# The first channel product of two more batches in 11 products for 12

## The chip, the cores and the metric

The kernel runs on one core of a Trainium2 chip. The metric is the device time of one execution in microseconds (us), as a median of several runs; the profile comes from one execution of its own. TensorE (PE) multiplies, VectorE (DVE) and ScalarE (ACT) work on what it leaves in PSUM, GpSimd (POOL) clears buffers and starts some transfers, SyncE (SP) starts the others. Each engine takes its instructions strictly in the order in which the program gives them.

## The reference

All arrays are float32: 4 batches, 8 heads, 768 tokens, head size 48, so 384 values per token.

```python
def attn(q, k, v, beta):                      # for each batch and head
    k_n = k / (norm(k) + 1e-6)
    for t in range(768):
        y[t] = q[t] @ state                   # state: 48 x 48
        v_old = state.T @ k_n[t]
        state = state + beta[t] * outer(k_n[t], v[t] - v_old)

x = y                                         # (batch, 768, 384), heads side by side
h = x.transpose(0, 2, 1) @ U @ V              # mixes tokens, rank 32
u = x + h.transpose(0, 2, 1)
ch = maximum(u @ w_ch1, 0) @ w_ch2            # 384 -> 1536 -> 384
out = u + ch
```

## The kernel before, in words

**Attention.** The recurrence is worked in chunks of 64 tokens. The eight (batch, half of the tokens) units n0 to n7 go through `grams` (transposes and products of keys and queries), `blocks` (a triangular substitution on VectorE, a chain of pairs of instructions, lines 803 and 809, between transposes at lines 794 and 816), `joins` (small products that put blocks of 32 together to 64) and `prepare`. `recur(b)` then runs over the twelve chunks of a batch, with the `z` subtraction (line 1085) and the state addition (line 1111) on VectorE between its products.

**Mixer.** For each batch b and each tile i of 256 tokens, `front(b, i)` mixes the tokens into X (line 1417) and transposes the tile (line 1436), and ScalarE copies it to `ut` (line 1439, two buffers). `wide(b, i)` then makes two channel products:

- The first, 384 to 1536, in `channels(e)` for e = 0 to 5 (batches 0 to 2). Each takes two of the twelve column blocks f of w_ch1, three matmuls of 128x128 weights by 256 tokens for each (line 1497). PSUM bank `mix` 0 or 1 holds the result; ScalarE applies relu into `hs` (line 1462, 512 columns at once).
- The second, 1536 to 384, in `narrow(e)` (line 1617): seven products in place of eight, by sums of the halves of `hs` (`add_up`, line 1524, and `last_sum`) and of the weights. `gather` adds the results to X (line 1537), SyncE stores them.

The last batch, b = 3, is different already: `quick(f)` makes its first product for all 768 tokens in 11 matmuls for 12, of 384 columns (line 1296). It uses sums of weights, made by `weight_sums` (lines 1256 and 1264: n1, s2 and s4, and a21 replaced by a11 - a21), and sums of the transposed tokens (`token_sums`, line 1280). Of each f and its partner f + 6, four results c(k, m) are built up: products run on in PSUM, ScalarE copies a state of the sum out (lines 1314, 1318, 1323), VectorE adds another product to it (line 1305), ScalarE applies relu (line 1300).

**Order.** Every function is a generator that gives one step of one engine at a time: `op(engine, cost, mode, take, give)`. A string named ORDER lists, for each generator, the places of its steps in the whole program; `run()` gives out the instructions in exactly that order. `need(...)` says which events have to have been given out before; `take` and `give` hand PSUM banks on. The cost in an `op` is a note of the program to itself, and no instruction depends on it. Modes say how TensorE's array is used: F is whole (128x128), Q is 64x64 or 48x64 parts, J 32x32 parts, T 128x32.

Of the kernel before, what the change touches and what calls it, by code (L numbers as in the profile page):

```python
# [20 lines left out]
GT = 256  # L21
# [6 lines left out]
def kernel(  # L28
# [66 lines left out]
    def dve(n):  # L95
        return (n + 151) / 960.0
# [48 lines left out]
    add_up b0 i0 f00: 573 585 613; add_up b0 i0 f03: 645 676 690; add_up b0 i1 f00: 795 797 800; add_up b0 i1 f03:  # L145
    818 819 824; add_up b0 i2 f00: 942 944 1042; add_up b0 i2 f03: 1023 1051 1071; add_up b1 i0 f00: 1161 1166 1186;
    add_up b1 i0 f03: 1189 1190 1191; add_up b1 i1 f00: 1309 1337 1363; add_up b1 i1 f03: 1357 1359 1368; add_up b1
    i2 f00: 1488 1493 1571; add_up b1 i2 f03: 1564 1572 1576; add_up b2 i0 f00: 1695 1717 1737; add_up b2 i0 f03:
    1728 1729 1730; add_up b2 i1 f00: 1888 1895 1906; add_up b2 i1 f03: 1886 1889 1901; add_up b2 i2 f00: 1992 2000
    2026; add_up b2 i2 f03: 2046 2047 2049; add_up b3 i0 f00: 2185 2186 2188; add_up b3 i0 f03: 2191 2192 2195;  # L150
    add_up b3 i1 f00: 2201 2202 2207; add_up b3 i1 f03: 2208 2209 2210; add_up b3 i2 f00: 2227 2228 2236; add_up b3
    i2 f03: 2224 2225 2229; blocks n0: 61 73 75 76 82 84 86 88 89 91 93 94 96 97 103 110 114 122; blocks n1: 143 157
    160 163 173 175 179 192 201 206 208 212 213 215 218 219 226 229; blocks n2: 479 496 501 502 508 512 513 514 515
    516 518 519 525 532 534 536 539 542; blocks n3: 704 720 721 729 730 733 739 741 761 765 769 771 772 773 778 779
    780 781 783 785 786 787 791 798 801 802 813 815 823 828 829 834 836 838; blocks n4: 971 982 985 987 989 996 1007
    1009 1012 1036 1038 1039 1040 1064 1074 1077 1082 1083 1087 1090 1107 1116 1119 1120 1122 1127 1129 1131 1132
    1133 1137 1138 1139 1140; blocks n5: 1168 1195 1198 1207 1218 1225 1227 1230 1231 1236 1241 1244 1249 1259 1269
    1271 1276 1278 1281 1286 1288 1291 1293 1294 1298 1311 1313 1314 1316 1323 1324 1332 1333 1351; blocks n6: 1510
    1523 1532 1541 1547 1558 1563 1566 1567 1568 1569 1596 1603 1612 1616 1617 1620 1622 1624 1645 1649 1653 1660
    1663 1665 1666 1671 1672 1673 1674 1675 1681 1684 1699; blocks n7: 1713 1724 1725 1739 1741 1744 1757 1762 1767  # L160
    1773 1775 1780 1782 1783 1800 1806 1807 1810 1817 1824 1829 1834 1837 1838 1849 1850 1856 1857 1860 1865 1866
    1867 1879 1881; both f0: 2149; both f1: 2105; both f2: 2147; both f3: 2123; both f4: 2111; both f5: 2184;
    channels b0 i0 e0: 546 547; channels b0 i0 e1: 549 550; channels b0 i0 e2: 552 553; channels b0 i0 e3: 567 574;
    channels b0 i0 e4: 588 591; channels b0 i0 e5: 604 633; channels b0 i1 e0: 768 776; channels b0 i1 e1: 777 788;
    channels b0 i1 e2: 790 792; channels b0 i1 e3: 799 803; channels b0 i1 e4: 806 807; channels b0 i1 e5: 808 814;
    channels b0 i2 e0: 898 899; channels b0 i2 e1: 907 912; channels b0 i2 e2: 935 936; channels b0 i2 e3: 950 959;
    channels b0 i2 e4: 965 969; channels b0 i2 e5: 995 1005; channels b1 i0 e0: 1118 1130; channels b1 i0 e1: 1136
    1148; channels b1 i0 e2: 1150 1151; channels b1 i0 e3: 1153 1155; channels b1 i0 e4: 1156 1158; channels b1 i0
    e5: 1159 1175; channels b1 i1 e0: 1297 1299; channels b1 i1 e1: 1300 1302; channels b1 i1 e2: 1304 1305; channels
    b1 i1 e3: 1306 1307; channels b1 i1 e4: 1326 1327; channels b1 i1 e5: 1342 1343; channels b1 i2 e0: 1430 1431;  # L170
    channels b1 i2 e1: 1432 1449; channels b1 i2 e2: 1450 1469; channels b1 i2 e3: 1470 1497; channels b1 i2 e4: 1498
    1501; channels b1 i2 e5: 1516 1530; channels b2 i0 e0: 1650 1654; channels b2 i0 e1: 1656 1669; channels b2 i0
    e2: 1686 1687; channels b2 i0 e3: 1689 1692; channels b2 i0 e4: 1697 1698; channels b2 i0 e5: 1700 1701; channels
    b2 i1 e0: 1808 1812; channels b2 i1 e1: 1813 1831; channels b2 i1 e2: 1833 1841; channels b2 i1 e3: 1843 1869;
    channels b2 i1 e4: 1871 1873; channels b2 i1 e5: 1874 1876; channels b2 i2 e0: 1950 1959; channels b2 i2 e1: 1960
    1961; channels b2 i2 e2: 1973 1979; channels b2 i2 e3: 1987 1999; channels b2 i2 e4: 2011 2027; channels b2 i2
    e5: 2033 2037; copies f0: 2127 2136; copies f1: 2082 2095; copies f2: 2129 2142; copies f3: 2086 2107; copies f4:
    2085 2103; copies f5: 2166 2168; cut f0 k0 to0: 2173; cut f0 k0 to1: 2169; cut f0 k1 to1: 2152; cut f1 k0 to0:
    2139; cut f1 k0 to1: 2106; cut f1 k1 to1: 2112; cut f2 k0 to0: 2153; cut f2 k0 to1: 2158; cut f2 k1 to1: 2163;
    cut f3 k0 to0: 2146; cut f3 k0 to1: 2154; cut f3 k1 to1: 2206; cut f4 k0 to0: 2171; cut f4 k0 to1: 2137; cut f4  # L180
    k1 to1: 2165; cut f5 k0 to0: 2181; cut f5 k0 to1: 2187; cut f5 k1 to1: 2194; diagonals n0 h0: 188 190 191 195 210
    222; diagonals n0 h1: 167 169 171 176 181 186; diagonals n1 h0: 312 315 319 336 343 353; diagonals n1 h1: 290 292
    303 338 349 358; diagonals n2 h0: 576 577 578 579 595 600; diagonals n2 h1: 632 646 665 670 705 707; diagonals n3
    h0: 854 855 860 865 870 873; diagonals n3 h1: 848 849 885 905 960 966; diagonals n4 h0: 1160 1162 1172 1197 1200
    1215; diagonals n4 h1: 1164 1192 1205 1211 1223 1226; diagonals n5 h0: 1356 1361 1365 1375 1402 1413; diagonals
    n5 h1: 1354 1380 1392 1419 1443 1444; diagonals n6 h0: 1708 1710 1711 1738 1745 1749; diagonals n6 h1: 1712 1723
    1726 1747 1753 1754; diagonals n7 h0: 1899 1905 1913 1931 1942 1945; diagonals n7 h1: 1892 1898 1911 1912 1918
    1957; first f0: 2160; first f1: 2097; first f2: 2135; first f3: 2138; first f4: 2092; first f5: 2180; front b0
    i0: 495 500 506 509 524 537; front b0 i1: 556 562 602 624; front b0 i2: 634 640 672 680; front b1 i0: 1055 1065
    1066 1078 1091 1111; front b1 i1: 1216 1224 1232 1237; front b1 i2: 1338 1348 1412 1425; front b2 i0: 1595 1599  # L190
    1605 1608 1623 1628; front b2 i1: 1633 1661 1702 1764; front b2 i2: 1801 1811 1835 1845; front b3 i0: 2041 2042
    2048 2050 2052 2054; front b3 i1: 2055 2061 2062 2067; front b3 i2: 2068 2070 2074 2076; gather b0 i0 h0 c0
    finalFalse: 671; gather b0 i0 h0 c0 finalTrue: 695; gather b0 i0 h0 c1 finalTrue: 756 1010; gather b0 i0 h1 c0
    finalFalse: 710; gather b0 i0 h1 c0 finalTrue: 757 805; gather b0 i0 h1 c1 finalFalse: 715; gather b0 i0 h1 c1
    finalTrue: 738; gather b0 i1 h0 c0 finalFalse: 820; gather b0 i1 h0 c0 finalTrue: 831; gather b0 i1 h0 c1
    finalTrue: 896 1061; gather b0 i1 h1 c0 finalFalse: 851; gather b0 i1 h1 c0 finalTrue: 881 1367; gather b0 i1 h1
    c1 finalFalse: 868; gather b0 i1 h1 c1 finalTrue: 867; gather b0 i2 h0 c0 finalFalse: 1017; gather b0 i2 h0 c0
    finalTrue: 1041; gather b0 i2 h0 c1 finalTrue: 1105 1185; gather b0 i2 h1 c0 finalFalse: 1079; gather b0 i2 h1 c0
    finalTrue: 1097 1163; gather b0 i2 h1 c1 finalFalse: 1084; gather b0 i2 h1 c1 finalTrue: 1086; gather b1 i0 h0 c0
    finalFalse: 1188; gather b1 i0 h0 c0 finalTrue: 1204; gather b1 i0 h0 c1 finalTrue: 1272 1778; gather b1 i0 h1 c0  # L200
    finalFalse: 1229; gather b1 i0 h1 c0 finalTrue: 1277 1591; gather b1 i0 h1 c1 finalFalse: 1238; gather b1 i0 h1
    c1 finalTrue: 1247; gather b1 i1 h0 c0 finalFalse: 1358; gather b1 i1 h0 c0 finalTrue: 1378; gather b1 i1 h0 c1
# [295 lines left out]
    S2 = const.tile([128, HF, 128], FP32, name="S2")  # L498
    X = const.tile([128, 2, NB, DM], FP32, name="X")
    clock["dve"], clock["pool"] = 4.7, 3.5  # L500

    TURNED = 3
    TURNED_K = 3
    SPLIT, QUARTERED = (0, 1), (2,)
# [1191 lines left out]
```

## Time and profile before

| | |
|---|---|
| median of 3 runs | 598.91 us (597.73 to 600.75) |
| profiled execution | 596.6 us, span 594.9 us |
| busy in the span | PE 559.7, PEld 481.6, DVE 409.3, ACT 216.8, POOL 133.3 us |
| first channel product, line 1497 | 648 passes of 256 columns, 150.1 us busy |
| second channel product, line 1617 | 1008 passes of 192 columns, 175.8 us busy |
| first product of the last batch, line 1296 | 132 passes of 384 columns, 42.7 us busy |

Lines are those of the kernel before. PE is the matmuls, PEld the weight loads beside them; a float32 matmul is recorded as two passes, each with a load. The time of a group is the union of its instructions, the mean of one includes the tail in the array, so a pass of a long group costs less than its mean. The first channel products of the nine tiles of batches 0 to 2 start at 116, 168, 202, 252, 292, 332, 380, 419 and 458 us; the last batch's starts at 507.

### The profile page before, as it was taken

To read this page: it belongs to the slowest core of one execution; us is meant where nothing else is said; L and a number is where in the kernel's file an instruction comes from. 1 tells how busy PE (TensorE), PEld (TensorE's weight loads), DVE (VectorE), ACT (ScalarE), POOL (GpSimd) and SP (SyncE) were. 2 spreads that over 40 slices of the span, in tenths; PEclk is the share of its full clock that TensorE was granted. 3 is DMA by queue.
4 is the path that set the end of the run, shared out by engine and by line. 5 is a ranking of instruction groups with operands and counts; after the bars stand their busy time and mean duration, and the time that the engine had idled before them with its cause. 6 is when DMAs were issued, how large, how long until landed. Compare 5 with 4: busy or idle time off the path is not lost.

```text
span 594.9 us, 23426 instructions
## 1 busy us (share of the span) xinstructions
PE 559.7 (94%) x10428; PEld 481.6 (81%) x10428; DVE 409.3 (69%) x1011; ACT 216.8 (36%) x442; POOL 133.3 (22%) x229
## 2 busy tenths in 40 slices
PE   3778978899999999999999999999999999999997
PEld 3578977678988887989889887889899868656997
DVE  3888758899999458999884279998883235313542
ACT  1846475446322542035224341252243321335000
POOL 8122036116010724141205214520310000000000
PEclk9855556999999999999999999999999999999999
DMA  9981639714030415240402144420401000000000
GB/s 140 180 176 24 214 80 197 152 56 79 3 65 12 68 31 92 46 91 13 82 2 43 18 83 90 79 56 2 95 7 43 4 2 4 16 8 1 26 28 28
DMA packets 89445, 36.23 MB, mean 61 GB/s; under 512 B 75456, under 2 KB 87104, under 8 KB 89344
## 3 DMA queue, kind: packets, MB, share of 16 engines
q1 hardware_dynamic: 80800, 24.69, 20.7%
q0 software_dynamic: 6944, 9.74, 8.3%
q8 instruction: 82, 1.34, 1.0%
q10 hardware_dynamic: 1600, 0.30, 0.3%
q14 instruction: 19, 0.16, 0.1%
HBM read 29.98 MB, written 4.72 MB: 58 GB/s over the span
## 4 chain that ended last, share of the span: by engine, by line
PE 83%; DVE 11%; issue 2%; ACT 2%; DMA 1%; SPq 0%; DVEq 0%; ACTq 0%
PE P L1617 27%; PE P L1497 22%; PE P L1296 7%; PE P L700 4%; DVE xt L809 3%; DVE prod L803 3%; PE P L1072 2%; PE P L860 2%; PE P L874 2%; PE P L1023 2%; PE P L1034 2%; PE P L983 2%; PE P L997 2%; PE P L1100 2%; PE P L1412 2%
## 5 line engine op out<-in xcount | busy, mean ns | idle before, releaser
L1497 PE MATMUL P<-ut,w_sb 128*128 128x256 f32 x648 | 150.1, 385 | 1.5 <-ACT ut L1439 0.9
L1497 PEld LDWEIGHTS P<-ut,w_sb 128*128 128x128 f32 x648 | 119.9, 190 | 18.7 <-ACT ut L1439 1.1
L1617 PE MATMUL P<-w_sb,hs 128*128 128x192 f32 x540 | 96.7, 331 | 0.1
L1617 PEld LDWEIGHTS P<-w_sb,hs 128*128 128x128 f32 x540 | 87.2, 190 | 3.7 <-issue 1.2
L809 DVE TENSOR_TENSOR xt<-xt,prod 128x112 f32<-128x112 f32 (+21 forms) x200 | 64.6, 323 | 6.9
L803 DVE TENSOR_TENSOR prod<-gs,xt 128x112 f32<-128x112 f32 (+21 forms) x200 | 63.3, 316 | 3.5
L1537 DVE TENSOR_TENSOR X<-X,P 128x192 f32<-128x192 f32 x84 | 29.1, 349 | 49.8 <-PE P L1617 49.4
L1462 ACT ACTIVATE hs<-P 128x512 f32<-128x512 f32 x54 | 32.2, 598 | 77.5 <-PE P L1497 65.6
L967 ACT COPY X<-P 64x192 f32<-64x192 f32 x96 | 30.0, 313 | 66.3 <-PE P L997 63.4
L1617 PE MATMUL P<-w_sb,S 128*128 128x192 f32 x288 | 50.7, 330 | 0.0
L1617 PEld LDWEIGHTS P<-w_sb,S 128*128 128x128 f32 x288 | 46.6, 190 | 2.8 <-issue 1.8
L555 POOL DMA_DIRECT2D slot<-in_v_dram x32 | 21.1, 664 | 92.3 <-DVE prod L803 60.3
L1085 DVE TENSOR_TENSOR z<-slot,P 128x192 f32<-128x192 f32 x44 | 15.5, 352 | 30.8 <-PE P L1072 29.7
L541 POOL DMA_DIRECT2D slot<-in_q_dram x40 | 24.6, 621 | 46.9 <-DVE slot L747 33.3
L939 ACT COPY slot<-zz 32x384 f32<-32x384 f32 x64 | 32.4, 509 | 7.0 <-DVE zz L878 3.9
L700 PE MATMUL P<-slot 48*64 48x64 f32 x1536 | 30.9, 231 | 2.1 <-issue 1.4
L1296 PE MATMUL P<-slot,w_sb 128*128 128x384 f32 x96 | 32.9, 486 | 0.0
L700 PEld LDWEIGHTS P<-slot 48*64 48x64 f32 x1536 | 27.9, 144 | 5.6 <-issue 2.7
L946 POOL MEMSET slot<- 32x384 f32 x32 | 13.3, 421 | 84.2 <-PE P L903 63.4
L1617 PE MATMUL P<-w_sb,slot 128*128 128x192 f32 x180 | 30.4, 327 | 0.9 <-DVE X L1537 0.9
L555 POOL DMA_DIRECT2D slot<-in_k_dram x44 | 29.4, 670 | 8.3 <-PE P L1100 7.6
L1617 PEld LDWEIGHTS P<-w_sb,slot 128*128 128x128 f32 x180 | 29.3, 190 | 1.7 <-DVE X L1537 1.5
(153 smaller groups left out, 901.4 us busy)
## 6 DMA issues: line engine op xcount, KB each, us to landing
out_dram<-X SPq DMA_DIRECT2D x22, 192.0 KB, 2.7
w_sb<-in_moe_w_ch_dram SPq DMA_DIRECT2D x10, 384.0 KB, 5.6
slot<-in_k_dram SPq DMA_DIRECT2D x48, 72.0 KB, 3.9
slot<-in_k_dram POOLq DMA_DIRECT2D x44, 72.0 KB, 3.8
slot<-in_v_dram SPq DMA_DIRECT2D x32, 72.0 KB, 3.7
slot<-in_v_dram POOLq DMA_DIRECT2D x32, 72.0 KB, 3.5
X<-in_moe_w_ch_dram SPq DMA_DIRECT2D x6, 384.0 KB, 6.1
wide<-in_moe_w_ch_dram SPq DMA_DIRECT2D x6, 384.0 KB, 5.0
```

Of the source, the lines that this page charges most:

```text
L541: queue.dma_start(out=blocked(n)[quarter(y % 4), j, g, :, 0:w], in_=src[b, 4 * g + 2 * j + par, hf * UC * L : (hf + 1) * UC * L, BK * low ...
L555: queue.dma_start(out=t[half(1 - g if name == "z" else g), :, to, 0:D], in_=src[b, 4 * g + s, hf * UC * L : (hf + 1) * UC * L, :].rearrang ...
L700: nc.tensor.matmul(p_g[half(g ^ (par * i)), par, c], kq[rows, c, j, 0, half(g)], kq[rows, c, j, i, half(g)], start=True, stop=True,)
L803: nc.vector.tensor_tensor(out=prod, in0=gb[:, :, j : j + 1, j + 1 :].to_broadcast([128, split, m, w]), in1=xb[:, :, 0:m, j : j + 1].to_bro ...
L809: nc.vector.tensor_tensor(out=xb[:, :, 0:m, j + 1 :], in0=xb[:, :, 0:m, j + 1 :], in1=prod, op=ALU.subtract,)
L939: nc.scalar.copy(pg[quarter(i), :, at, :, a : a + BK], cut(zc, h)[quarter(i)].rearrange("p r (c j) t -> p r c j t", j=2),)
L967: nc.scalar.copy(x[half(c % 2), c // 2, 4 * D * g : 4 * D * (g + 1)].rearrange("p (j r d) -> p r j d", r=2, d=D), states(p_y)[half(g)],)
L1296: nc.tensor.matmul(to, w, t, start=start, stop=stop, skip_group_check=True)
L1462: nc.scalar.activation(hs[:, fs[0] : fs[1] + 1 : fs[1] - fs[0]], p_f, ACTF.Relu)
L1497: nc.tensor.matmul(p_f[:, x], w(x, t), ut[:, t], start=(t == 0), stop=(t == KT - 1))
L1537: nc.vector.tensor_tensor(out=to, in0=to, in1=p, op=ALU.add)
L1617: nc.tensor.matmul(to, of[0], of[1], start=of[2], stop=of[3], skip_group_check=True)
```

## The change

The first channel product of batches 1 and 2, FROM = (1, 0) on, is also made in 11 products for 12. The unit is a tile of 256 tokens as two halves of 128: `tile_sums(b, i)` makes the sums of the tokens (four VectorE instructions), and `brisk(f0)`, for f0 = 0 and 3, takes the place of three of the six `channels`. A step of it is one of the 11 products for three f at once: three matmuls of 128 columns into one PSUM bank (384 columns). The steps of a half tile run one after the other in the two banks `px` and `pz`, with copies, additions and relus of 384 columns in between as in `quick`. The next half begins when the first is done.

Beside it: `weight_sums` no longer waits for batch 1 and changes a21 after the last tile of batch 0; `ut` has one buffer and not two, and `front` waits for the first product of the tile before only ahead of its transposes; `narrow` takes the parts of `hs` by the new events. ORDER is a new one throughout (2259 steps before, 2427 after); it is left out here. The comments in the diff are added to number the steps.

```diff
+    FROM = (1, 0)
...
     def weight_sums():
-        yield need(("weights", W2 + 5), ("narrow", 1, 0))
+        yield need(("weights", W2 + 5))
...
-        yield need(("wide", LAST - 1, NG - 1))
+        yield need(("wide", *before(*FROM)))
...
     def front(b, i):
         yield need(
-            ("front", *before(b, i)), *[("wide", *before(*before(b, i)))] * (b < LAST),
+            ("front", *before(b, i)),
...
-            ut = uts[b, i] = mix.tile([128, KT, GT], FP32, name="ut")
+            ut = uts[b, i] = mix.tile([128, KT, GT], FP32, name="ut", bufs=1)
+            if (b, i) >= FROM:
+                t_sums[b, i] = mix.tile([128, 4, 128], FP32, name="ts", bufs=1)
...
+        if b < LAST:
+            yield need(("wide", *before(b, i)))
         plain = op("pe", 0.655, "F", take="pair", words=12, flow=0.64)
...
+    def tile_sums(b, i):
+        yield need(("front", b, i))
+        u = uts[b, i].rearrange("p t (m n) -> p t m n", m=2)
+        ts = t_sums[b, i]
+        for size, to, a, c, how in (
+            (256, ts[:, 0:2], u[:, 0::2, 0], u[:, 0::2, 1], ALU.subtract),
+            (128, ts[:, 2], u[:, 1, 1], ts[:, 0], ALU.add),
+            (128, u[:, 0, 1], u[:, 1, 1], u[:, 0, 1], ALU.subtract),
+            (128, ts[:, 3], u[:, 1, 0], ts[:, 2], ALU.subtract),
+        ):
+            yield op("dve", dve(size), port=True)
+            nc.vector.tensor_tensor(out=to, in0=a, in1=c, op=how)
+        emitted(("tokens", b, i), 0.1)
...
+        def brisk(f0):
...
+            def mm(to, ws, t, start=False, stop=False):
+                for x in range(3):
+                    of = ws[x] if isinstance(ws, list) else ws[:, x]
+                    nc.tensor.matmul(to[:, x], of, t, start=start and x == 0, stop=stop, skip_group_check=True)
...
+            def cut(k, to):                       # relu in place
+                yield op("act", act(384))
+                nc.scalar.activation(c(k, to), c(k, to), ACTF.Relu)
...
+            def add(k, m, p, **more):
+                yield op("dve", dve(384), rush=True, **more)
+                nc.vector.tensor_tensor(out=c(k, m), in0=c(k, m), in1=p, op=ALU.add)
+                begin(cut(k, m), 3)
...
+            mm(px, w(0, 0), u(0, 0), start=True, stop=True)       # step 1
+            begin(copies(), 3)                                    # ACT: c00 <- px; later c11 <- pz
...
+            mm(pz, w(0, 1), u(1, 0), start=True)                  # 2
...
+            mm(pz, w(0, 2), u(2, 0), stop=True)                   # 3
+            begin(first(), 3)                                     # DVE: c00 += pz
+            yield need(("tokens", b, i), ("w1 sums", 1), ("begun", b, i, f0))
...
+            mm(px, s2, t2, stop=True)                             # 4
+            begin(second(), 3)                                    # ACT: c01 <- px
+            yield need(("start", b, i, f0))                       # the addition of first()
...
+            mm(pz, n1, t1, start=True, stop=True)                 # 5
+            yield need(("second", b, i, f0), ("w1 sums", 0))
...
+            mm(px, w(1, 0), u(0, 1))                              # 6
...
+            mm(px, w(1, 2), u(2, 1), stop=True)                   # 7
+            begin(crossing(), 3)                                  # DVE: c11 += px
+            yield need(("third", b, i, f0))                       # ACT: c11 <- pz
...
+            mm(pz, s4, u(1, 1))                                   # 8
...
+            mm(pz, w(0, 2), u(2, 1), stop=True)                   # 9
+            begin(both(), 3)                                      # DVE: c01 += pz
+            yield need(("crossed", b, i, f0))                     # the addition of crossing()
...
+            mm(px, w(1, 1), t4)                                   # 10
...
+            mm(px, w(1, 2), t5, stop=True)                        # 11
...
+            yield op("act", act(384), rush=True, give=[("mix", 0)])
+            nc.scalar.activation(c(1, 0), px, ACTF.Relu)
...
             emitted(("wide", b, i))
+        elif (b, i) >= FROM:
+            begin(brisk(0), 95)
         else:
             for e in range(len(PAIRS)):
                 begin(channels(e), 95)
```

## The prediction

> **What bounds the kernel now.** I read the page first, for which engine is full and when.
>
> ```profile
> PE 559.7 (94%) x10428; PEld 481.6 (81%) x10428; DVE 409.3 (69%) x1011; ACT 216.8 (36%) x442; POOL 133.3 (22%) x229
> ...
> PE   3778978899999999999999999999999999999997
> PEld 3578977678988887989889887889899868656997
> DVE  3888758899999458999884279998883235313542
> ```
>
> From the ninth slice (about 120 us) TensorE is full, nearly to the end. So a product that is taken out there is worth its time, unless TensorE then waits. VectorE is full in three long stretches. The windows show them in the region that the change touches (columns: length, then busy us of PE, weight loads, DVE, ACT, POOL; granted clock; DMA share; GB/s):
>
> ```profile
> 250.00:300.00 50.00, 49.92 (x883) 44.73 (x882) 45.95 (x119) 18.48 (x36) 15.36 (x25) 1.00 0.29 58
> 300.00:350.00 50.00, 49.94 (x1072) 44.06 (x1071) 26.84 (x63) 19.93 (x41) 13.91 (x24) 1.00 0.24 42
> 350.00:400.00 50.00, 49.74 (x750) 41.99 (x748) 47.29 (x126) 15.84 (x34) 19.09 (x32) 1.00 0.34 66
> 400.00:450.00 50.00, 49.43 (x1023) 44.40 (x1022) 42.56 (x110) 18.16 (x37) 8.19 (x15) 1.00 0.15 33
> 450.00:507.00 57.00, 56.96 (x934) 46.78 (x934) 18.89 (x49) 14.29 (x32) 0.00 (x0) 1.00 0.05 16
> ```
>
> DVE has room at 300 to 350 and after 450, and next to none at 250 to 300 and 350 to 400. Today that does not hurt: the products of lines 1497 and 1617 fill TensorE whatever DVE does. Then the chain, in order of time, for the price of one pass (a float32 matmul is recorded as two passes):
>
> ```profile
> 252.29 15.74 PE P L1497 x72
> ...
> 506.88 42.57 PE P L1296 x132
> 549.45 13.66 PE P L1617 x84
> ```
>
> A pass of 384 columns costs 42.57/132 = 0.3225 us, one of 192 columns 13.66/84 = 0.1626. The straight line through both gives 0.216 at 256 columns (the first row: 72 x 0.216 = 15.55 and 0.19 for its start) and **0.1093 at 128**. Last the timeline of one group, for the loads and for the change of array shape:
>
> ```profile
> 304.51 2.46 PEld L1497 LDWEIGHTS P<-ut,w_sb 128*128 128x128 f32 x12
> 304.51 2.86 PE L1497 MATMUL P<-ut,w_sb 128*128 128x256 f32 x12
> ...
> 307.30 0.45 PE L1072 MATMUL P<-s,slot 48*64 48x48 f32 x16
> ```
>
> Twelve loads span 2.46 = 10 x 0.216 + 0.190 (one load) + 0.108: the first two stand 0.108 apart, which is what a load occupies. The matmuls span 2.86 = 11 x 0.216 + 0.379 (one) + 0.104: the first waited for its load.
>
> **The products.** A tile loses 36 matmuls of 256 columns: 72 x 0.216 = 15.55 us. It gets 22 steps of three matmuls of 128 columns: 132 x 0.1093 = 14.43. Six tiles: **-6.7 us**. No row has ordinary 128-column passes. Below, 0.1093 is held by the load (0.108), which just hides; above, by 0.1626, since a 192-column pass with the same load costs that. I take 0.1093, as every row from 192 to 384 columns lies on the line.
>
> The Trainium skill (TensorE: Matmul & The Clock Gate, "LDWEIGHTS") gives a load 128/1.2 = 107 ns, with which the 108 here agrees; its "Back-to-back issue gap" has streams of load and matmul at 128 columns at 81 ns where the bare gap is 56, so 25 ns more. By that a pass would cost an estimated 0.134 and the six tiles +12.9 us instead of -6.7; no run here shows it.
>
> **Changes of shape.** The orders in the text can be counted. Steps where TensorE leaves the full 128x128 form: 78 before, 83 after; changes between the 64- and 32-row forms: 12 and 21. In the trace leaving costs 0.093 (from 304.51, 12 passes and the 0.104 end at 307.21; the next starts at 307.30), coming back 0.11, and the first load stands bare, 0.104: 0.30 us a round. 5 x 0.30 + 9 x 0.11 = **+2.5 us**. Both ends: 1.0 (the nine cost nothing) and 3.5.
>
> **ScalarE.** A tile has 14 copies and relus of 384 (0.48 to 0.52) for 6 relus of 512 (0.598): 20 us in all on an engine 36% busy; hidden, but a product now waits for it. From a product's last pass streamed to the next that needs the copy: 0.164 tail, 0.04 to start, 0.48, about 0.07 back: 0.75. Where only one step (0.656) stands between, which I count five times, 0.1 is lost; where step one of the second half follows the last relu at once (b1 i0) 0.75. **+1.25 us**, between 0.5 (copies answer at once) and 3.5 (each of the larger ACT bursts in the order is met).
>
> **VectorE.** 36 additions of 0.555 and 24 token sums (0.41 or 0.285) are added: 27.6 us, of which each new one overlaps its neighbour by 0.08 in the trace: about 22.6 of queue time. 24 weight sums of 0.285 move from batches 1 to 3 into batch 0, beside products; uncovered they would cost 6.8. The new thing is that step 5 and step 10 of each half tile **wait for an addition that stands in DVE's queue behind the substitution**; TensorE's queue behind them (recurrence, joins, second product) waits too. So between two such points the time is the longer of both queues. I summed both from the order with the trace's durations (a substitution pair 0.3 to 0.8, L794 1.97, L816 2.10, a 16-pass group 0.26). The same sums on the order of before give TensorE 387 us from the first channel product to the last batch's, where 391 went by. Stage by stage, TensorE/DVE, from one tile's first product to the next's:
> before b1: 39.8/44.7, 39.7/19.0, 47.3/37.0; b2: 37.9/38.2, 39.8/26.6, 48.1/14.0;
> after b1: 38.9/38.2, 40.2/30.5, 44.9/37.5; b2: 37.0/37.9, 41.0/31.5, 47.0/17.6.
> DVE now nearly equals TensorE in b1 i0 and passes it in b2 i0. Point by point: from the crossing addition of b1 i0's first half to the first of its second, DVE holds 2.10 + 1.97 + 4 x 0.41 + 0.555 less overlaps = 5.76 and its own 0.56; TensorE has 3.94 and 1.64 in hand: 0.74 lost. From b1 i2 to b2 i0: 27.98 + 0.56 against 25.82 + 1.72: 1.0 lost. Six smaller ones: 1.5. **+3.2 us**; 0.6 if DVE has run ahead, 16 if each addition waits for all that stands between it and its product.
>
> **Rest.** One buffer of transposed tokens: a tile's six transposes (0.8), copy (0.8) and sums (1.2) now follow the last product of the tile before; seven narrow products of 1.95 cover them (2.8 a tile if not). No DMA is added; SP and POOL have 226 and 218 steps in both orders.
>
> **Sum.** -6.7 + 2.5 + 1.25 + 3.2 = +0.25 on the profiled execution (span 594.9, 596.6 in all), which is 2.3 below the median of 598.9. Forecast: **599 us, no change** (within 0.5%, 3 us, about what a measurement of this kernel can tell from none). Its own range is 596 to 602.
>
> **Rivals.**
> *A, faster: the additions come in time.* DVE's queue is strict, but before, of 36 recurrence waits whose additions stood behind 31 us of such work by the order, TensorE lost only 5.3 us: DVE was ahead. Then VectorE costs 0.6 and the sum is -6.7 + 2.5 + 1.25 + 0.6 = -2.4; with the low ends of shapes and ScalarE -4.6: 594.3 to 596.5, say 595. Against it: now DVE must come back twice in every half tile, so it can't run ahead. 0.30.
> *B, slower: VectorE sets the pace.* If DVE lags at the points where its queue is full, half to all of the 16 us are lost: +5 to +13, say 607. It decides once DVE's sum passes TensorE's in most stages: 5% dearer instructions put b1 i0 and b2 i0 over by 1 to 3 us each. For it: 47.29 of 50 busy at 350 to 400. 0.20.
> *C, slower: the load shows.* If a 128-column stream can't hide a load and a pass costs the middle of 0.109 and 0.163, 0.136, six tiles change by +14.4 instead of -6.7; TensorE then gives DVE time and the waits shrink to about 1: 14.4 + 2.5 + 1 = 17.9, so 617. Against it: the 0.108 above. The issue-gap rule of the Trainium skill, cited above, would be this mechanism. 0.10.
> The change may also not do what it says; the text excludes that: 66 against 72 units a tile.
>
> **How the numbers follow.** Forecast 0.40, A 0.30, B 0.20, C 0.10. Faster by over 0.5%: A, 0.30. Same: 0.40. Slower: B and C, 0.30. The range takes in A with its low end (594.3, and 2 us for a stage order that wins more) and B's middle: 592 to 608; left out are C and the far end of B.
>
> **What would show it.** Right: 792 passes of 128 columns about 0.109 apart; three batches' first products as before; DVE at 45 or more of 50 us from 250 to 400; idle rows of PE before the new matmuls, released by DVE, of 2 to 4 us in all. A shows none of those; B shows over 8 us of them, in b1 i0 and b2 i0; C shows passes 0.12 or more apart with no wait named. The forecast is wrong if TensorE's wait lies elsewhere, as in batch 0 behind the moved weight sums.

## The result and the profile after

Over 20 runs of each, the changed kernel takes **602.75 us** (600.02 to 606.39) and the kernel before 598.36 (596.26 to 602.38): ratio **1.0072 [1.0051, 1.0092]**, 4.4 us slower. The sum had said +0.25. Its single steps follow further down; first the profile, in the views in which the kernel before was read.

The page of the changed kernel:

```profile
span 601.6 us, 24280 instructions
...
PE 562.8 (94%) x10788; PEld 496.4 (83%) x10788; DVE 429.6 (71%) x1071; ACT 235.2 (39%) x490; POOL 133.3 (22%) x229
...
PE   4697987899999999999999998999999999999997
PEld 3596876687989987999999996989999978655997
DVE  3879866899999689988986488999994235222542
...
PEclk9756655999999999999999999999999999999999
```

Busy time says little here: TensorE has 3.1 us more of it although a product in twelve is gone, but that is the union of its instructions with their tails, and it has the first 120 us in it. The weight loads grew by 14.8 us, since there are 360 more. Of the 6.7 us between the two spans, 3.1 lie ahead of the first channel product, which starts at 119.05 and not at 115.9. There the granted clock (the row PEclk; that of the kernel before follows) is low for some slices and comes up sooner or later from one execution to the next. In the three profiles with the old order (before, experiments 1 and 6) this lead is 113.9 to 115.9 us long, in the eight with the new one 115.6 to 120.3. It is 114 to 116 where the granted clock was 0.5 for 65 to 68 us of it, and 118 to 120 where it was so for 75 to 85. Whether the new order lengthens it, and with it makes some of the 4.4 us, is not shown.

```profile
PEclk9855556999999999999999999999999999999999
```

So the profiles are compared from the first channel product on. What repeats there can be read off the eight profiles with the new order: their batch 0 takes 134.3 to 135.2 us, their last batch 88.83 to 88.85. To the first product of batch 1, of the last batch, and to the end:

| us | batch 0 | batches 1 and 2 | last batch | together |
|---|---|---|---|---|
| before | 136.3 | 254.5 | 88.2 | 478.9 |
| after | 134.9 | 258.8 | 88.8 | 482.6 (+3.6) |

The windows of the changed kernel (columns as before: length, busy us of PE, weight loads, DVE, ACT, POOL, granted clock, DMA share, GB/s):

```profile
250.00:300.00 50.00, 48.63 (x923) 45.35 (x922) 45.15 (x118) 20.81 (x43) 17.18 (x28) 1.00 0.25 56
300.00:350.00 50.00, 49.62 (x1146) 46.66 (x1145) 31.45 (x77) 24.26 (x53) 12.64 (x22) 1.00 0.26 51
350.00:400.00 50.00, 47.69 (x758) 43.09 (x750) 46.24 (x125) 15.33 (x36) 11.34 (x18) 1.00 0.30 53
400.00:450.00 50.00, 49.59 (x1004) 46.28 (x1002) 46.89 (x122) 23.70 (x51) 14.32 (x24) 1.00 0.19 42
450.00:507.00 57.00, 56.90 (x1186) 50.22 (x1177) 23.05 (x52) 20.81 (x47) 1.65 (x4) 1.00 0.03 10
```

The first and the third hold the loss: TensorE is busy 48.63 and 47.69 of 50 us, where it had 49.92 and 49.74. VectorE has 45 to 47 us there as before, but now something waits for it. The chain in order of time (start, length, engine, what) gives the pace of the new product:

```profile
267.20 4.97 PE P L1562 x42
...
512.93 28.39 PE P L1311 x88
...
555.99 13.84 PE P L1764 x84
```

42 passes in 4.97 us: less the first load, which stands bare, with no matmul running beside it (0.104), and the last pass whole (0.279, the mean of one below), 4.59 are left for 41 starts, **0.112 us a pass**. Start to start in the whole trace, 474 of the intervals are 112 ns and 238 are 111; the mean is 0.1117. L1311 is `quick` and L1764 the second channel product: they run at their old pace (28.39/88 = 0.3226, 13.84/84 = 0.165; start to start a pass of 192 columns takes 0.162 or 0.163, as before). The costliest groups by line, shapes apart (mean ns of one, then the idle time ahead of them and what ended it):

```profile
L1562 PE MATMUL P<-ut,w_sb 128*128 128x128 f32 x432 | 56.3, 279 | 1.7 <-DVE X L1681 1.1 <-ACT hs L1650 0.6
L1562 PE MATMUL P<-ts,wide 128*128 128x128 f32 x144 | 21.0, 284 | 0.2
```

And the timeline where the first tile of batch 1 begins (start, length, engine, what, in brackets the idle time before it and what ended it):

```profile
253.46 0.35 DVE L1681 TENSOR_TENSOR X<-X,P 128x192 f32<-128x192 f32 x1 [0.69 <-PE P L1764]
253.96 2.25 PE L1562 MATMUL P<-ut,w_sb 128*128 128x128 f32 x18 [0.54 <-DVE X L1681]
256.04 1.81 PE L1562 MATMUL P<-ts,wide 128*128 128x128 f32 x12
256.31 0.55 DVE L1574 TENSOR_TENSOR hs<-hs,P 128x384 f32<-128x384 f32 x1 [0.19 <-PE P L1562]
257.69 1.50 PE L1562 MATMUL P<-ut,w_sb 128*128 128x128 f32 x12
```

Step one takes a PSUM bank that held a second product, so it waits until `gather` (L1681) has added that to X: 0.54 us idle, and its first load after that. Then steps 2 to 4 run on, and VectorE's first addition (L1574) begins 0.19 after its product's end. Step 5 must wait for it, 0.21 us from start to start, about half of it its bare first load.

I added up the changed kernel's time in batches 1 and 2 from start to start of TensorE's instructions, and the same for the kernel before:

| us in batches 1 and 2 | before | after | |
|---|---|---|---|
| passes of the first product | 432 x 0.216 = 93.3 | 792 x 0.11167 = 88.4 | -4.9 |
| first loads that stand bare, 0.1 each | 5.0 (49) | 6.0 (60) | +1.0 |
| leaving the whole array, coming back, between part shapes | 11.1 | 12.8 | +1.7 |
| work in 64- and 32-row parts | 51.3 | 52.9 | +1.6 |
| waits | 6.2 | 10.8 | +4.6 |
| the rest | 87.6 | 87.9 | +0.3 |

The fourth row is work that the new order moved out of batch 0 (there 32.2 to 30.6). Over the whole: passes -4.9; shapes and bare loads +3.6 (2.7, and 0.9 in batch 0); waits +3.9 (4.6, and -0.7 in batch 0); last batch +0.65; rest +0.3; that is the +3.6 above. How much of a slow stretch is called a wait depends on how one sorts; the windows over batches 1 and 2 give the idle time alone, 254.50 - 253.49 = 1.0 us before and 258.81 - 254.78 = 4.0 after:

```profile
252.22:506.72 254.50, 253.49 (x4559) 219.83 (x4553) 179.18 (x458) 86.71 (x179) 55.30 (x93) 1.00 0.21 43
```

```profile
253.96:512.77 258.81, 254.78 (x5008) 234.19 (x5009) 193.09 (x487) 105.70 (x227) 57.13 (x96) 1.00 0.20 41
```

### The profile page after: what moved, and what is told of

The parts are those of the page before. It is cut to its first block, busy times and chain, and to the rows that moved or that the text cites. A ratio compares the mean times of both kernels' runs of the same rounds, so it can differ in the third digit from the quotient of the medians.

```text
span 601.6 us, 24280 instructions
## 1 busy us (share of the span) xinstructions
PE 562.8 (94%) x10788; PEld 496.4 (83%) x10788; DVE 429.6 (71%) x1071; ACT 235.2 (39%) x490; POOL 133.3 (22%) x229
## 4 chain that ended last, share of the span: by engine, by line
PE 80%; DVE 9%; ACT 4%; issue 3%; DMA 2%; SPq 1%; POOL 0%; DVEq 0%; ACTq 0%
PE P L1764 28%; PE P L1562 14%; PE P L1311 7%; PE P L1533 6%; PE P L715 4%; PE P L1087 2%; PE P L998 2%; PE P L1049 2%; PE P L875 2%; PE P L1038 2%; PE P L1115 2%; PE P L1012 2%; PE P L889 2%; DVE xt L824 1%; PE P L1455 1%
## 5 line engine op out<-in xcount | busy, mean ns | idle before, releaser
L1764 PE MATMUL P<-w_sb,hs 128*128 128x192 f32 x540 | 95.9, 330 | 0.0
L1764 PEld LDWEIGHTS P<-w_sb,hs 128*128 128x128 f32 x540 | 87.1, 190 | 2.9 <-issue 0.6
L1562 PE MATMUL P<-ut,w_sb 128*128 128x128 f32 x432 | 56.3, 279 | 1.7 <-DVE X L1681 1.1
L1681 DVE TENSOR_TENSOR X<-X,P 128x192 f32<-128x192 f32 x84 | 29.1, 349 | 38.0 <-PE P L1764 37.8
L1562 PEld LDWEIGHTS P<-ut,w_sb 128*128 128x128 f32 x432 | 51.2, 192 | 3.3 <-issue 1.6
L1533 PE MATMUL P<-ut,w_sb 128*128 128x256 f32 x216 | 50.4, 386 | 0.9 <-ACT ut L1458 0.9
L1764 PE MATMUL P<-w_sb,S 128*128 128x192 f32 x288 | 50.3, 328 | 0.0
L1764 PEld LDWEIGHTS P<-w_sb,S 128*128 128x128 f32 x288 | 46.7, 190 | 2.0 <-issue 1.2
L1533 PEld LDWEIGHTS P<-ut,w_sb 128*128 128x128 f32 x216 | 39.9, 190 | 6.6 <-ACT ut L1458 1.1
L556 POOL DMA_DIRECT2D slot<-in_k_dram x40 | 24.7, 625 | 53.8 <-DVE z L1100 25.6
L1311 PE MATMUL P<-slot,w_sb 128*128 128x384 f32 x96 | 33.2, 487 | 0.2 <-ACT slot L1338 0.2
L715 PE MATMUL P<-slot 48*64 48x64 f32 x1536 | 32.2, 238 | 1.3 <-issue 1.3
L715 PEld LDWEIGHTS P<-slot 48*64 48x64 f32 x1536 | 29.0, 150 | 4.7 <-issue 3.1
L1320 DVE TENSOR_TENSOR slot<-slot,P 128x384 f32<-128x384 f32 x18 | 9.4, 552 | 31.4 <-PE P L1311 31.4
L1764 PE MATMUL P<-w_sb,slot 128*128 128x192 f32 x180 | 30.5, 328 | 0.9 <-DVE X L1681 0.9
L1764 PEld LDWEIGHTS P<-w_sb,slot 128*128 128x128 f32 x180 | 29.3, 190 | 2.0 <-DVE X L1681 1.5
```

Of the source, the lines that this page charges most:

```text
L556: queue.dma_start(out=blocked(n)[quarter(y % 4), j, g, :, 0:w], in_=src[b, 4 * g + 2 * j + par, hf * UC * L : (hf + 1) * UC * L, BK * low ...
L715: nc.tensor.matmul(p_g[half(g ^ (par * i)), par, c], kq[rows, c, j, 0, half(g)], kq[rows, c, j, i, half(g)], start=True, stop=True,)
L1311: nc.tensor.matmul(to, w, t, start=start, stop=stop, skip_group_check=True)
L1533: nc.tensor.matmul(p_f[:, x], w(x, t), ut[:, t], start=(t == 0), stop=(t == KT - 1))
L1562: nc.tensor.matmul(to[:, x], of, t, start=start and x == 0, stop=stop, skip_group_check=True)
L1681: nc.vector.tensor_tensor(out=to, in0=to, in1=p, op=ALU.add)
```

## Experiments

The theories. **P**: the pass of 128 columns is paced by its load at 0.1117, against the straight line of the prediction (0.1093). **W**: the loss is the waits in the new product, one by one as the trace names them. **V**: VectorE's queue is so full that what is taken from one wait comes back at the next. **O**: the new order costs time whatever the product.

**1. Only the passes.** The kernel before in its own order; each matmul of 256 columns in batches 1 and 2 in two of 128.

```diff
-                        nc.tensor.matmul(
-                            p_f[:, x], w(x, t), ut[:, t], start=(t == 0), stop=(t == KT - 1)
-                        )
+                        for z in range(2 if b else 1):
+                            at = slice(128 * z, 128 * z + 128) if b else slice(0, GT)
+                            nc.tensor.matmul(
+                                p_f[:, x, at], w(x, t), ut[:, t, at],
+                                start=(t == 0 and z == 0), stop=(t == KT - 1), skip_group_check=True,
+                            )
```

> The kernel before, its order untouched; only each 256-column matmul of the first channel product of batches 1 and 2 is split into two of 128 columns with the same weights loaded twice (864 passes of 128 for 432 of 256). It prices the pass alone, without any new wait. Theory P (a pass of 128 columns is paced by its weight load, 111.6 ns as the changed kernel's profile shows in its rows): 864 x 0.1116 - 432 x 0.216 = +3.1 us, so about 601.5. Theory of the prediction (0.1093): +1.1 us, 599.5. If a pass had a dearer price when nothing else shapes the stream, over +6 us.

Measured: 603.12 us beside 598.83, ratio 1.0072 [1.0044, 1.0101]; batches 1 and 2 take 257.8 us, 3.3 more. Its chain in order of time:

```profile
257.08 16.27 PE P L1499 x144
...
297.67 10.91 PE P L1499 x96
```

The 144 half passes take 16.27 where the 72 whole ones took 15.74: 0.53 us a tile, 3.2 for six. That is P; by the straight line it would be 1.1, below the interval of the ratio. (In this execution batch 0 is 5.5 us longer than before: the granted clock was 0.5 for 6.8 us there. Batches 1 and 2 have 1.00 throughout.) With no new wait and no new order, the pass alone behaves as in the changed kernel.

**2. Fewer columns.** In the changed kernel each matmul of the new product takes 96 columns of 128.

```diff
-                    nc.tensor.matmul(to[:, x], of, t, start=start and x == 0, stop=stop, skip_group_check=True)
+                    nc.tensor.matmul(to[:, x, 0:96], of, t[:, 0:96], start=start and x == 0, stop=stop, skip_group_check=True)
```

> The changed kernel, same order; only each matmul of the new first product takes 96 of its 128 columns (a quarter of the product is missing). Theory P (a pass of 128 columns is paced by its load): the pass stays at 111 to 112 ns and the time within 1.5 us of the changed kernel's. Theory of the straight line through 192, 256 and 384 columns: 0.083 us a pass, 792 x 0.028 = -22 us, less what then becomes waits.

Measured: 601.66 us, ratio to the kernel before 1.0041 [1.0016, 1.0066]; batches 1 and 2 257.4 us, 1.4 less than in the changed kernel, of which next to nothing lies in the passes (0.4 is a shorter wait at L715, treated under "Last batch and rest"). Its chain, and its group:

```profile
263.81 4.94 PE P L1562 x42
```

```profile
L1562 PE MATMUL P<-ut,w_sb 128*128 128x96 f32 x432 | 55.8, 278 | 1.7 <-DVE X L1681 1.1 <-ACT hs L1650 0.6
```

A quarter of the columns is gone, and 42 passes take 4.94 for 4.97; start to start it is 112 (478 times) and 111 ns (234 times), as with 128. So at 128 columns not the columns are paid but the load. The Trainium skill (TensorE: Matmul & The Clock Gate, "LDWEIGHTS") puts such a load at 128/1.2 = 107 ns; the 0.1117 is that and 4 to 5 ns more. The estimate of 0.134 that followed from its "Back-to-back issue gap" is not borne out by any of these rows.

The traces hold a check from the other side. The transposes of a tile (L1436 before, L1455 after) are passes of 128 columns too, but each of their loads takes 140 ns, where those of L1562 take 186 to 192. Six of them in the chain, and their loads:

```profile
246.91 0.66 PE P L1455 x6
```

```profile
L1455 PEld LDWEIGHTS P<-ident,X 128*128 128x128 f32 x72 | 8.4, 140 | 0.4
```

They start 0.109 apart, on the straight line. So the line does reach 128 columns, and it is the ordinary load that lifts the new product's pass off it.

**3. No waits.** In the changed kernel, the copies, the additions and the last relu read a constant and not the bank; their number, size and place stay. What they give is not the product's.

```diff
+            still = v_sb[:, 0:384].rearrange("p (x n) -> p x n", x=3)
...
-                nc.vector.tensor_tensor(out=c(k, m), in0=c(k, m), in1=p, op=ALU.add)
+                nc.vector.tensor_tensor(out=c(k, m), in0=c(k, m), in1=still, op=ALU.add)
...
-                nc.scalar.copy(c(0, 0), px)
+                nc.scalar.copy(c(0, 0), still)
...
```

> The changed kernel, same order, same count of instructions on every engine; only the copies and relus of ScalarE and the additions of VectorE in the new first product read a constant in SBUF in place of the PSUM bank, so TensorE waits for none of them (the values are then not the product's). Theory W (the loss is the waits inside the new product): the stalls ahead of the new matmuls, 2.7 us in the trace, and with each of them a bare first load of 0.1, about 12 to 20 of them, go: 598 to 599, -4 us. Theory V (VectorE's queue, fuller by some 22 us, makes others wait): load kept, so less than -2 us. Theory O (the new order itself: more changes of shape, other waits, 3 us lost ahead of 120 us): less than -2 us as well.

**4. No extra work.** The same instructions left out altogether, with the other relus and the sums of the tokens; the matmuls stay.

```diff
-                nc.vector.tensor_tensor(out=c(k, m), in0=c(k, m), in1=p, op=ALU.add)
+                pass
...
-                nc.scalar.copy(c(0, 0), px)
+                pass
...
-            t1, t5, t2, t4 = (t_sums[b, i][:, z] for z in range(4))
+            t1, t5, t2, t4 = (ut[:, z % 3, 0:128] for z in range(4))
...
```

> The changed kernel, same order and same matmuls; the copies, additions and relus of the new first product and its token sums are left out (their values are missing, and the token sums are replaced by tokens). So VectorE has 60 and ScalarE 84 instructions less. Theory W: the same as without the waits, 598 to 599. Theory V: about 3 us below that, 595 to 596, since the stalls of the recurrence, joins and grams that grew by 2.8 us shrink back. Theory O: no better than without the waits.

Measured: 600.31 us, ratio 1.0025 [0.9994, 1.0055], and 599.77 us, 1.0014 [0.9987, 1.0041]. Batches 1 and 2 take 255.9 and 254.6 us. So the waits of the new product for its copies, additions and relus, with what follows from them, cost 258.8 - 255.9 = 2.9 us. The two waits of step one for `gather` (0.70 each from start to start) stay in both runs. The load on VectorE and ScalarE costs at most another 1.3: the medians do not separate the two runs, and 0.6 of the 1.3 is one wait at L715 (1.27 us in the first trace, 0.63 in the second) that VectorE and ScalarE do not end. And even with neither, a stretch in which TensorE has 4.9 us less of first product takes as long as before (254.5): 5 us went elsewhere, 1.6 of them the work moved from batch 0. What is left points to O.

**5. The order alone.** The new order with the old product (`FROM = (3, 0)`): the `channels` stand at the places of the `brisk` steps, the relus behind them.

```diff
-    FROM = (1, 0)
+    FROM = (3, 0)
```

> The new order with the old first product: in the places of the new steps stand the six channel products of 12 in 256 columns with their relus, as before the change; copies, additions and token sums are gone, and the last six weight sums are again ahead of the last batch. What is left of the change is the order of all else, and the single buffer of transposed tokens. Theory O (the order costs 3 to 5 us by itself: changes of shape, waits elsewhere): 602 to 604, no better than the changed kernel. Theory W (the new product's waits are the loss, the order is harmless): 598 to 599.5, as before.

Measured: 611.40 us, 1.0206 [1.0171, 1.0240], slower than the changed kernel itself. The waits of TensorE in it say why that settles nothing:

```profile
PE P L1068 <- ACT slot L716: 1.4, 1, 1.4
...
PE P L1068 <- ACT slot L1043: 1.3, 2, 0.9
```

I had put the relus so early in ScalarE's queue that it stood at them, while the copies for the recurrence (L716, L1043) were queued behind and TensorE waited for those. With the relus later in the queue:

> The new order with the old first product once more; now each relu of 512 stands later in ScalarE's queue, at the place where the changed kernel has one of its own copies or relus of that half tile, so that ScalarE does not stand at a product that is still to come while copies for the recurrence queue up behind it. Theory O (the order costs 4 to 6 us by itself, as the run without the extra work suggests): 602 to 605. Theory W (the order is harmless): 598 to 600. If it stays near 611, ScalarE's queue was not the reason there, and the old product doesn't fit the new order at all.

Measured: 602.73 us beside 599.89, ratio **1.0052 [1.0018, 1.0086]**: +2.8. Batches 1 and 2 take 259.3 us, 4.8 more than before, batch 0 134.9 and the last 88.8, both as in the changed kernel. So the order by itself costs about 3 us by the medians (4.2 from its one trace), and the new product in that order changes next to nothing: -4.9 of passes, +2.9 of waits, up to +1.3 of load. The ratios 1.0052 and 1.0072 can't be told apart. The waits of TensorE in this run hold a row that the changed kernel has too:

```profile
PE P L1514 <- DVE X L1662: 1.1, 2, 0.5
```

L1514 is the old product, L1662 `gather`. So the two waits for a bank of the second product are the order's, and would be there without the new product. This is an upper bound for the order: it was written for the new product, and another place for the old steps in it may be better.

**6. The product in the old order.** The changed kernel with the old ORDER; the `brisk` steps at the places of the `channels`.

> The other way round: the whole new first product, with its sums and single buffer, in the order of before. Two steps stand where one channel step of 256 columns stood, copies and additions right behind the steps they read, relus a step or two later; the weight sums are spread over the last tile of batch 0; all else keeps its old order. Theory O: the passes save 4.9 us, the waits inside the product cost 3 to 5, the old order costs nothing: 597 to 599, faster than the changed kernel by 4 or more. Theory W: an order that was not made for these steps makes the waits worse: 603 to 608.

Measured: **668.06 us**, ratio 1.1138 [1.1095, 1.1180]; batches 1 and 2 322.2 us, TensorE idle for 322.20 - 279.71 = 42.5 of them. Neither expectation was near. Its waits of TensorE (sum, number, longest), and its windows, the last over both batches:

```profile
PE P L1557 <- DVE hs L1569: 18.1, 8, 5.6
...
PE P L1759 <- ACT hs L1645: 4.2, 2, 3.5
...
PE P L1557 <- ACT hs L1645: 3.1, 5, 0.6
```

```profile
253.00:300.00 47.00, 37.03 (x596) 34.31 (x595) 33.42 (x83) 17.37 (x36) 8.59 (x15) 0.85 0.14 30
300.00:350.00 50.00, 40.73 (x733) 37.16 (x734) 33.82 (x84) 15.10 (x37) 7.37 (x12) 0.90 0.16 31
...
251.40:573.60 322.20, 279.71 (x4920) 252.68 (x4913) 199.21 (x494) 105.46 (x227) 55.31 (x94) 0.92 0.17 34
```

The product (there L1557) stands up to 5.6 us for one addition (L1569) that is queued behind the substitution, and with TensorE standing VectorE starves in turn: 33 of 47 us busy. The old order lets VectorE lag (in the prediction's table 44.7 us against TensorE's 39.8 in the first tile of batch 1), which the old product never noticed. So the new order is no mere by-product: the new product needs VectorE up to date. That keeping it so takes the more and smaller groups on TensorE that the new order has is an inference. Only this one placement was run, with the steps put by rule where the old ones stood; a better one in the old order may cost less. The granted clock was 0.5 for 54.6 of the 322.2 us besides, where it is 1.00 before and after, so some of the time lost is not the waits themselves.

**7. Other banks.** In the changed kernel, the two banks of the new product change roles in the first tiles of batches 1 and 2, so that step one takes a bank that is free earlier.

```diff
+            lead = {(1, 0, 0): 1, (2, 0, 0): 1, (2, 0, 3): 1}.get((b, i, f0), 0)
...
-            yield op("pe", 0.64, "F", take=("mix", 0), words=12)
-            px, pz = (mixed(z)[:, 0:384].rearrange("p (x n) -> p x n", x=3) for z in range(2))
+            yield op("pe", 0.64, "F", take=("mix", lead), words=12)
+            px, pz = (mixed(z)[:, 0:384].rearrange("p (x n) -> p x n", x=3) for z in (lead, 1 - lead))
...
```

> The changed kernel, same order and same instructions; only in the tiles b1 i0 and b2 i0 the two PSUM banks of a half tile are swapped where step 1 stood still for 0.70 to 0.74 us (twice behind the last addition of the second product, once behind the last relu of the half before), so that step 1 takes the bank that came free earlier. Theory W (waits inside the new product): three waits of 0.7 shrink to 0.1 each, -1.8 us: 600.5 to 601. Theory O (order, shapes): TensorE reaches its next wait earlier and stands there instead: no change, within 1 us of 602.75.

Measured: 601.56 us beside 598.74, ratio 1.0047 [1.0021, 1.0074]; batches 1 and 2 258.5 us, 0.3 less, and batch 0, which ends where the first of the three waits ended, 134.3, 0.6 less. The waits at step one went from 0.70, 0.74 and 0.70 us to 0, 0.28 and 0. Its timeline at the first tile of batch 1:

```profile
253.38 2.22 PE L1563 MATMUL P<-ut,w_sb 128*128 128x128 f32 x18
255.44 0.83 PE L1563 MATMUL P<-ts,wide 128*128 128x128 f32 x6
256.18 0.52 DVE L1575 TENSOR_TENSOR hs<-hs,P 128x384 f32<-128x384 f32 x1
256.75 0.94 PE L1563 MATMUL P<-ts,wide 128*128 128x128 f32 x6 [0.47 <-DVE hs L1575]
```

Step one starts at once, and step 5 pays: it stands 0.47 us idle until VectorE's addition is done (its wait grew from 0.21 to 0.64 us, in batch 2 from 0.21 to 0.76). Of the 1.9 us that step one gave up, 1.0 came back at step 5, the next place where VectorE's queue is met; the other 0.9 were won (0.6 + 0.3). So the truth lies between V, which would have had all of it come back, and W, which would have had none; the medians of the two kernels differ by too little to say more.

**8. More on VectorE.** One more addition of the same size behind each of the 36, that nobody waits for.

```diff
                 nc.vector.tensor_tensor(out=c(k, m), in0=c(k, m), in1=p, op=ALU.add)
...
+                nc.vector.tensor_tensor(out=spare, in0=still, in1=still, op=ALU.add)
```

> The changed kernel, same order; behind each of the 36 additions of the new first product VectorE does one more of the same size on a constant, into a buffer that nobody reads: 36 x 0.47 = 17 us more in VectorE's queue. The prediction's sum of both queues (VectorE equal to TensorE in b1 i0, above it in b2 i0) makes TensorE wait for nearly all that falls there and in b1 i2 and b2 i1: +6 to +10 us, 609 to 613. If VectorE in fact runs ahead of its additions, as the trace after suggests (step 5 stood still for no more than 0.21): under +3 us.

Measured: 609.45 us, ratio 1.0168 [1.0140, 1.0195]; batches 1 and 2 264.7 us, 5.9 more than in the changed kernel, for 17 us of VectorE work (36 x 0.472, what one adds beside its overlapping neighbour). Its windows where VectorE is full:

```profile
250.00:300.00 50.00, 48.35 (x918) 44.97 (x917) 47.23 (x124) 20.17 (x41) 16.84 (x28) 1.00 0.24 51
...
400.00:450.00 50.00, 48.60 (x978) 44.74 (x978) 48.53 (x128) 22.57 (x47) 15.33 (x25) 1.00 0.19 43
```

A third of the added work shows. So VectorE is not the bound everywhere, but in the full stretches it is at the edge: it goes to 47 and 48.5 of 50 us and takes TensorE's time with it.

Taken together: P is shown, by experiments 1 and 2 and the transposes. W is right for about 3 us. V is right in part: half of what was taken from one wait came back, and a third of what was added showed. O is right for up to 4.2 us, in which the two waits for `gather` are.

## Why the prediction was right and wrong, step by step

The forecast was no change, 599 us, with the range 592 to 608; it came out 0.7% slower, inside the range and outside the 0.5%. It fell between the forecast and rival B by a sum that none of the four had. The terms of the sum, in us:

| term | predicted | measured |
|---|---|---|
| passes | -6.7 | -4.9 |
| shapes, bare loads | +2.5 | +3.6, some 1.0 of it first loads after waits |
| ScalarE and VectorE waits | +1.25 and +3.2 | all waits +3.9; of these 0.7 at the new product's relu, 0.8 at its additions |
| last batch and rest | 0 | +0.95 |

Of the 3.4 us between +0.25 and +3.6, the passes make 1.8, shapes and bare loads 1.1, last batch and rest 0.95; the waits take 0.5 off.

**The passes are the step that failed.** "As every row from 192 to 384 columns lies on the line": so they do, but the line ends where the load begins. The prediction had the bound in hand (0.108 from the two loads that stand alone), and let it "just hide" at 0.1093. Measured, each load and its successor stand 0.1117 apart, and the columns no longer count (experiments 1 and 2). 792 x 0.0024 = 1.9 us of the gain was never there. What makes 0.1117 out of 0.108 is open.

**Shapes** came out at what was counted from the order text: 2.6 without the first loads that follow a wait. The prediction had no term for those: the first pass after a wait or a change of shape takes 377 ns and not 275, so it costs 0.1 on top.

**ScalarE**: the expected 0.75 at step one of the second half in the first tile of batch 1 is there, 0.74 from start to start behind the relu (L1650), 0.6 of it idle; its other waits there came to at most 0.2 together. The waits of TensorE that belong to step one (us in total, times, longest), and from the view of the new product's line the idle time ahead of step 5, which is that of the weight loads:

```profile
PE P L1562 <- DVE X L1681: 1.1, 2, 0.5
...
PE P L1562 <- ACT hs L1650: 0.6, 1, 0.6
```

```profile
  DVE hs L1574: 0.9, 4
```

**VectorE**: the mechanism is there, the size and the places were wrong. Step 5 waits for its addition in four of the twelve half tiles, 0.84 us from start to start in all (the 0.9 of the row above), and step 10 in none; 3.2 was expected for both. Not foreseen were the two waits of step one for the `gather` of a second product (L1681), 1.4 from start to start. They go by way of a PSUM bank and not of an addition, and by experiment 5 they belong to the order. At two of the four places step 5 waited so little because TensorE had waited just before (experiment 7), and experiment 8 shows how little slack VectorE has left in the full stretches.

**Last batch and rest**: the prediction had batch 3 unchanged. A wait of 0.38 from start to start for ScalarE (L1338) and three bare loads came into it. One wait of batch 1 lies in the middle of a group of small transposes, and no semaphore released it:

```profile
368.45 0.34 PE L715 MATMUL P<-slot 48*64 48x64 f32 x6 [1.25 <-issue]
```

It makes up 1.25 of the 2.05 us that the third window lost. What it waited for can be read from the page's DMA queues and TensorE's instruction stream:

```profile
q8 instruction: 84, 1.38, 1.0%
```

84 packets of 16 KB for 21669 recorded instructions of TensorE, 82 for 20937 before: one for each 256 or so. After 100 us, the eleven profiles have 24 idle times of TensorE over 0.2 us that no semaphore ended. Each of the 24 lies at place 193 or 194 of a block of 256 (counted from 0), and 1.2 to 1.7 us after such a packet ended. That points to TensorE waiting there for its own instructions; it is read from the traces, and no run tried it. In batches 1 and 2 these waits are 1.5 us in the changed kernel and 0.6 before.

**Rivals.** A (the additions come in time, 595) had the size of VectorE's waits nearly right, 0.6 for 0.84, and fell by its time: experiment 4 shows that even without any additions the time is not below that of before. B (VectorE sets the pace) did not come about in this order; experiment 8 shows that 17 us more on VectorE bring 5.9, the low end of its price, and experiment 6 lies beyond its far end. C (the load shows) was there in small, 0.1117 for its 0.136.

The tests named for the forecast: 792 passes yes, 0.109 no. Idle rows of PE before the new matmuls, released by VectorE, are 1.1 of the "2 to 4", and 2.0 with the short ones that only the loads show. VectorE has 45 or more of 50 from 250 to 400 only in the first and third window (45.15, 46.24; 31.45 between). "TensorE's wait lies elsewhere" is half true: about 3 of the 10.8 us lie in the new product, 1.4 of them by the order. The 24 weight sums that moved into batch 0 cost nothing there: its waits fell from 5.3 to 4.6.

The order's price was in the prediction in part, as its changes of shape: TensorE leaves the whole array 71 times in batches 0 to 2 before, 76 in the changed kernel and 75 in the order alone. Not in it were the waits that the order itself makes, the two for `gather` above all, and the +0.65 in the last batch, which the order alone has too. Experiments 5 and 6 say what the order is worth: at most about 4 us for one in which VectorE is nearly current, against 42.5 us of idle TensorE in the one placement tried in which it lags.

## What to carry to other kernels

Before fewer and narrower matmuls are counted as a gain, look for the width at which the weight load sets the pace: here it is reached at 128 columns, and 11 products in halves save a quarter less than the count says (4.9 of 6.7 us). A product that comes back to another engine's queue in its middle has a second price, that this queue has to be current at each return; look in the trace how far it lags today, for the old code may hide a lag that the new one meets in full (up to 5.6 us at a time here). When the new order is part of the change, run it with the old work: here it costs up to 4.2 us for 4.9 of passes. And an idle time that no semaphore ends may be the engine's wait for its instructions: compare its place in the stream with the packets of the instruction queue.

## What was not expected of the hardware

- In the changed kernel a float32 pass of 128x128 weights and 128 columns came 0.111 to 0.112 us after the one before, all 712 times that neither a wait nor a change of shape lay between, and with 96 columns the same; at 192 columns it is 0.1626. The two loads that stand alone in the trace are 0.108 apart. Transposes, with loads of 140 ns for 190, come 0.109 apart at 128 columns.
- After a wait or a change of shape the first pass of the new product took 377 ns and not 275 (38 times).
- TensorE was idle for up to 1.25 us in groups of small matmuls with no releaser in the trace, always at the same place in a block of 256 instructions, 1.2 to 1.7 us after a packet of its instruction queue.
- In experiment 6, where TensorE stood for long, the granted clock was 0.5 for 54.6 us of batches 1 and 2, where the kernels before and after have none. Whether the waits caused it was not tried.
